# Hash attention with a squared-ReLU network on one core: the first pair of heads loads six tokens in a row per partition, transposes them by products, and the first weights' rounding moves to its usual place

## The chip, the cores and the metric

The kernel runs on one core of one Trainium2 chip. The metric is the device time of one execution in microseconds (us). Below, PE is TensorE, DVE is VectorE, ACT is ScalarE, POOL is GpSimd and SP is SyncE, as the profile names them; SPq and ACTq are transfers that SP and ACT issue. L396 is line 396 of the kernel.

## The reference

Attention for 4 batches of 8 heads, with 768 tokens of 64 features each. A token has six hash bits, the signs of its products with `proj`; a query attends only to keys with the same six bits.

```python
q_bits = (np.einsum('bhsd,dk->bhsk', q, proj) > 0)      # the same for k
mask = q_bucket[:, :, :, None] == k_bucket[:, :, None, :]
scores = np.where(mask, scale * np.matmul(q, k.T), -1e9)
attn = exp(scores - max) ; attn = attn / (sum(attn) + 1e-9)
x = (attn @ v), as 3072 tokens x 512 features
out = (maximum(x @ w_in, 0) ** 2) @ w_out                # 512 -> 2048 -> 512
```

`q`, `k`, `v` and `proj` are float32. `w_in` and `w_out` come as 64-bit floats and are rounded to float32 on the chip.

## The kernel before

The first part is the attention. It works through 16 pairs of heads; a pair fills 128 rows with its two heads' 64 features. The order of all instructions is written out by hand (`tc.manual_schedule()`), so each engine runs its instructions in the order of the text. The second part is the network. Its products run by a scheme with sums of blocks (L716, L888, L935), and it starts when the last pair is done. The first part holds about 317 us of the span.

One pair `pr` goes through these steps, and the names matter later:

- `load_pair` brings queries and keys of a pair (`q_nat`, `k_nat`) in 32-by-32 blocks. `features(pr, w)` transposes them on DVE (L333). `load_values` brings `v_nat`.
- `hash_bits` (L346) multiplies the features by the hash vectors on PE; `signs` (L356) makes the signs on ACT, 8 instructions a pair; `weigh` (L382) scales the key bits. `prepare` does hash and signs of the next pair. It is called inside `finish(pr - 1)`, after the second key tile of pair `pr`.
- `score(pr, kt)` computes the products of one key tile (128 keys) with all 768 queries: per column group, `bits` products and `feat` products accumulate in one tile of the pool `turn`, and one exponential on ACT (L413) takes them to `e`. A key tile has two column groups (512 and 256 queries, two heads each), thus two `turn` tiles and two exponentials. The pool has three buffers, shared by `score`, `hash_bits`, `sum_up` and the transposes of the first pair. A product that needs the fourth tile waits until the first has been read.
- `add_up` (L423, L428) sums the exponentials on DVE. `attend` (L438) multiplies them by the values. `sum_up`, `spread` and `normalize` end the pair; `finish(pr - 1)` runs the end of a pair inside the next one.

Between these steps the 64-bit network weights are rounded, two pieces per pair: `load_weight(i)` loads a piece (`raw`), `part_weight` splits its high word on DVE (L143, L147), `place_power` rebuilds the exponent on ACT (L160, L161), and `round_weight` puts it together on DVE (L171, L176, L179). In every pair but the first, `place_power(a)` and `round_weight(a)` of the even piece stand after the fourth key tile's exponentials. In pair 0 both stand behind the sixth key tile, after `weigh(1)`.

The first pair starts otherwise. `load_first` loads `q` and `k` in pieces of 128 tokens (token `t * 128 + p` on partition `p`), so a run in memory is one token, 256 bytes. `first_features(w, r)` transposes three pieces of both heads on PE, one 128 by 128 transpose each, and copies the result to `feat` (queries on ACT, L316; keys on DVE, L318). `keep_busy(n)` puts `n` unused products on PE (L326): eight before the first transposes and two between those of the queries and those of the keys. Then come the hash products, the signs of the queries on ACT, and `first_keys`, which makes the key bits on DVE (L370, L374).

Of the kernel before, what the change touches and what calls it, by code (L numbers as in the profile page):

```python
# [8 lines left out]
FP32 = mybir.dt.float32  # L9
# [25 lines left out]
def kernel(  # L35
# [10 lines left out]
    nc = tc.nc  # L46
    PSUM = bass.MemoryType.PSUM

    B, H, S, D = q.shape
# [3 lines left out]
    P = 128  # L53
    SB = S // P
    HS = S // 2
# [15 lines left out]
    ident = glob.tile([P, P], FP32, name="ident")  # L71
# [20 lines left out]
    p_qk = first.enter_context(tc.tile_pool(name="p_qk", bufs=2))  # L92
# [11 lines left out]
    def turn(name):  # L104

        return ps_s.tile([P, 2, 512], FP32, name=name, tag="turn")
# [11 lines left out]
    def goal(i):  # L118
        if i < 2 * NIN:
            return ins[i // NIN][:, i % NIN // 2, i % 2]  # L120
        return p_t.tile([P, DM], FP32, name="out_piece", bufs=3)
# [31 lines left out]
    def place_power(i):  # L153


        if i not in parts:
            return
        power = parts[i][0]
        small = p_w.tile([P, PIECE], U8, name="small")
        nc.scalar.activation(out=small, in_=power, func=ACTF.Relu, bias=excess)  # L160
        nc.scalar.activation(out=power, in_=small, func=ACTF.Copy, scale=2.0**23)  # L161

    def round_weight(i):

        raw = raws.pop(i, None)
        if raw is None:
            return keep_weight(i)
        goals[i] = goal(i)
        low, high = raw[:, :, 0], raw[:, :, 1]
        power, top = parts.pop(i)  # L170
        nc.vector.scalar_tensor_tensor(  # L171
            out=power, in0=high, scalar=0x80000000, in1=power,
            op0=ALU.bitwise_and, op1=ALU.bitwise_or,
        )
        one = top.bitcast(FP32)
        nc.vector.scalar_tensor_tensor(  # L176
            out=one, in0=low, scalar=2.0**-32, in1=top, op0=ALU.mult, op1=ALU.add,
        )
        nc.vector.scalar_tensor_tensor(  # L179
            out=goals[i], in0=one, scalar=2.0**-20, in1=power.bitcast(FP32),  # L180
            op0=ALU.mult, op1=ALU.mult,
        )
        keep_weight(i)

    def keep_weight(i):

        t = goals.pop(i)
        j, c = divmod(i, NIN)
        if j >= 2:
            nc.sync.dma_start(out=w_out_1[:, i - 2 * NIN], in_=t)  # L190
        elif c == NIN - 1:
            nf = NFT // 2
            for n, f, h in (0, 0, 0), (1, nf, 0), (2, nf, 1):
                put_factor(n, j * PIECE, ins[j][:, f:f + nf, h])
            nc.sync.dma_start(
                out=w_in_21[:, :, j * PIECE:(j + 1) * PIECE], in_=ins[j][:, 0:nf, 1]
            )
# [67 lines left out]
    nat, feat, bits = {}, {}, {}  # L265

    def load_first():

        for src, name in ((q, "q_nat"), (k, "k_nat")):
            t = p_qk.tile([P, SB, 2, D], FP32, name=name)  # L270
            for h, queue in enumerate((nc.sync, nc.scalar)):
                queue.dma_start(
                    out=t[:, :, h], in_=src[0, h].rearrange("(t p) d -> p t d", t=SB)
                )
            nat[0, name] = t
        for h, queue in enumerate((nc.sync, nc.scalar)):
            queue.dma_start(out=projs[h * D:(h + 1) * D, 0:NBITS], in_=proj)
# [15 lines left out]
    def load_values(pr):  # L293
        b, j = divmod(pr, PB)
        t = p_v.tile([P, 2, SB * D], FP32, name="v_nat")
        nc.sync.dma_start(
            out=t.rearrange("p h (t d) -> p (h t) d", d=D),
            in_=v[b, 2 * j:2 * j + 2].rearrange("h (t p) d -> p (h t) d", t=SB),
        )
        nat[pr, "v_nat"] = t  # L300

    def first_features(w, r):

        if r == 0:
            feat[0, w] = p_f.tile([P, S], FP32, name=f"feat{w}")
        tp = turn("tp")[:, 0]
        for i in range(SB // 2):
            t = r * (SB // 2) + i
            nc.tensor.transpose(  # L309
                out=tp[:, i * P:(i + 1) * P],  # L310
                in_=nat[0, ("q_nat", "k_nat")[w]][:, t].rearrange("p h d -> p (h d)"),
                identity=ident,
            )
        out = feat[0, w][:, r * HS:(r + 1) * HS]
        if w == 0:
            nc.scalar.copy(out=out, in_=tp[:, 0:HS])  # L316
        else:
            nc.vector.tensor_copy(out=out, in_=tp[:, 0:HS])  # L318

    busy = const.tile([P, 512], BF16, name="busy")  # L320
    void = ps_o.tile([P, 1024], FP32, name="xo")
# [1 line left out]
    def keep_busy(n, w=512):  # L323

        for _ in range(n):
            nc.tensor.matmul(  # L326
                out=void[:, 0:w], lhsT=busy[:, 0:P], rhs=busy[:, 0:w], start=True, stop=True
            )
# [8 lines left out]
    def hash_bits(pr, banks, ws=(0, 1), cs=(0, 1)):  # L337


        for w in ws:  # L340
            hashed[pr, w] = banks
            for c in cs:
                g = 2 * w + c
                for h in range(2):
                    rows = slice(h * D, (h + 1) * D)
                    nc.tensor.matmul(  # L346
                        out=banks[g * NR_B:(g + 1) * NR_B, h, 0:HS], lhsT=projs[rows],
                        rhs=feat[pr, w][rows, c * HS:(c + 1) * HS], start=True, stop=True,
                    )

    def signs(pr, w):
        bits[pr, w] = t = all_bits[pr % 2][w]
        for c in range(2):
            at = slice((2 * w + c) * NR_B, (2 * w + c + 1) * NR_B)
            for h in range(2):
                nc.scalar.activation(  # L356
                    out=t[h * D:h * D + NR_B, c * HS:(c + 1) * HS], in_=hashed[pr, w][at, h, 0:HS],
                    func=ACTF.Sign, scale=HUGE, bias=lifts[at],
                )
# [191 lines left out]
    def load_x(i):  # L551

        x = p_c.tile([P, NFT, NCH], FP32, name="x")
        nc.gpsimd.dma_start(out=x, in_=x_all[:, :, i * NCH:(i + 1) * NCH])
        xs[i] = x, [p_c.tile([P, 2, NCH // 2], FP32, name=f"t_x{n}") for n in range(3)]
# [36 lines left out]
    with tc.manual_schedule():  # L592
        nc.vector.memset(busy, 1.0)
        nc.vector.memset(projs, 0.0)
        load_first()
        keep_busy(8)
        make_identity(nc, ident)
        constants()
        load_pair(1)
# [2 lines left out]
            load_weight(i)  # L602
        first_features(0, 0)
        first_features(0, 1)
        keep_busy(2)
        first_features(1, 0)
        hash_bits(0, void.rearrange("p (h c) -> p h c", h=2), (0,))
        signs(0, 0)
# [5 lines left out]
        for pr in range(NP):  # L614
            a, b = 2 * pr, 2 * pr + 1
            more = pr + 1 < NP

            def prepare():

                hash_bits(pr + 1, turn("hash"))  # L620
                for w in (1, 0):
                    signs(pr + 1, w)


            if pr + 2 < NP:
                load_pair(pr + 2)
            if pr == X_0:
                load_x(0)
            if more and pr > 0:
                for w in range(2):  # L630
                    features(pr + 1, w)
            if pr > 0:
                round_weight(b - 2)
                load_weight(b)
                for m in sums.get(pr, ()):
                    sum_in(m)
            score(pr, 0)
            if pr == 0:
                first_keys(1, turn("hash"))
            score(pr, 1)  # L640
            if pr == 0:
                for w in range(2):
                    features(1, w)
            if pr > 0:
                finish(pr - 1, prepare if more else None)
            add_up(pr, 1)
            if pr > 0:
                normalize(pr - 1)


            if pr == X_0 + 1:
                for n in range(2):
                    load_unit(n)
            part_weight(a)
            score(pr, 2)
            if pr == 0:
                prepare()
            score(pr, 3)
            if more and pr > 0:
                weigh(pr + 1)  # L660
            if pr > 0:
                place_power(a)
            attend(pr, 0)
            attend(pr, 1)
            for kt in (2, 3):
                add_up(pr, kt)
            if more:
                load_values(pr + 1)


            if pr > 0:
                round_weight(a)
            part_weight(b)
            if more:
                load_weight(a + 2)
            score(pr, 4)
            score(pr, 5)
            if pr == 0:
                weigh(1)
                place_power(0)  # L680
                round_weight(0)
            place_power(b)
            attend(pr, 2)
            attend(pr, 3)
            add_up(pr, 4)
            add_up(pr, 5)
# [529 lines left out]
        for i in range(NCHUNK):  # L1216
            for s in range(NR):
                r = order(i * NR + s)
# [269 lines left out]
```

## Time and profile before

| | before |
|---|---|
| median of 3 runs | 884.32 us (882.99 to 885.01) |
| the profiled execution's own time | 884.32 us |
| its span | 882.6 us |
| mean granted TensorE clock | 0.993 |
| PE busy | 867.5 us (98% of the span) |
| DVE busy | 760.0 us (86%) |
| ACT busy | 391.5 us (44%) |

The span is the time from the first to the last instruction. It is 1.7 us shorter than the execution's own time; that remainder lies around the program. Busy shares are means over both parts of the kernel, so they don't say what bounds the short stretch in which the first pair runs. A row of a timeline gives the start, the length of a group of instructions, the engine, the line, the operation, the count, and in brackets how long the engine stood idle before it and what ended that.

### The profile page before, as it was taken

How to read it: one execution, taken by the hardware profiler on the slowest of the kernel's cores; microseconds unless marked ns; L12 is line 12 of the kernel's file. 1: busy time of each engine (PE TensorE's matmuls, PEld its weight loads, DVE VectorE, ACT ScalarE, POOL GpSimd, SP SyncE). 2: the span in 40 equal slices, each digit the busy share in tenths (PEclk: the TensorE clock that was granted, in tenths of full speed). 3: DMA queues.
4: the chain of work that ended last, by engine and by line, in shares of the span. 5: the costliest groups of instructions: out<-in, count | busy, mean ns of one | idle time of the engine just before them, and what ended most of it. 6: DMA issues, size and time to landing. Idle time of an engine off the chain costs nothing.

```text
span 882.6 us, 12133 instructions
## 1 busy us (share of the span) xinstructions
PE 867.5 (98%) x4340; PEld 520.6 (59%) x4340; DVE 760.0 (86%) x1099; ACT 391.5 (44%) x673; POOL 107.0 (12%) x172
## 2 busy tenths in 40 slices
PE   8899999999999999999999999999999999999996
PEld 4344444444444444444688875556888755568885
DVE  5799999999999998888779978888889788888875
ACT  6688888888888862222211123332111233321110
POOL 2000000000000000564222021111100211110002
PEclk9899999999999999999999999999999999999998
DMA  9567968899988634989897774436847744454565
GB/s 174 101 133 145 249 145 164 163 277 209 189 172 190 200 126 156 324 262 289 283 359 244 188 165 163 164 116 229 294 144 186 173 155 157 130 166 148 162 167 111
DMA packets 224131, 167.09 MB, mean 189 GB/s; under 512 B 164448, under 2 KB 181344, under 8 KB 224064
## 3 DMA queue, kind: packets, MB, share of 16 engines
q1 hardware_dynamic: 189152, 87.19, 41.1%
q0 software_dynamic: 12528, 41.30, 14.9%
q10 hardware_dynamic: 22384, 37.76, 14.2%
q8 instruction: 36, 0.59, 0.3%
q14 instruction: 31, 0.25, 0.1%
HBM read 124.52 MB, written 41.68 MB: 188 GB/s over the span
## 4 chain that ended last, share of the span: by engine, by line
PE 95%; DVE 2%; SPq 1%; DMA 1%; issue 0%; ACT 0%; DVEq 0%
PE acc L716 40%; PE st L396 16%; PE acc L935 16%; PE xo L438 13%; PE acc L888 5%; PE hash L346 2%; PE tot L455 1%; SPq L287 1%; DVE total L428 1%; DMA w_in<-s_in 1%; PE xo L326 0%; DMA raw<-in_moe_w_in_dram 0%; PE tp L309 0%; SPq L130 0%; PE xo L477 0%
## 5 line engine op out<-in xcount | busy, mean ns | idle before, releaser
L413 ACT ACTIVATE e<-st 128x1024 f32<-128x1024 f32 x192 | 145.0, 810 | 45.9 <-PE st L396 42.2
L396 PE MATMUL st<-feat,feat 64*128 64x512 f32 (+1 forms) x768 | 150.4, 484 | 0.0
L438 PE MATMUL xo<-e,v_nat 128*64 128x512 f32 (+1 forms) x768 | 136.0, 496 | 0.0
L716 PE MATMUL acc<-b,leaf 128*128 128x256 f32 x600 | 133.2, 379 | 0.5 <-issue 0.5
L716 PEld LDWEIGHTS acc<-b,leaf 128*128 128x128 f32 x600 | 113.9, 190 | 16.7 <-issue 1.5
L428 DVE TENSOR_TENSOR total<-total,e 128x1536 f32<-128x1536 f32 x64 | 112.4, 1756 | 8.4 <-ACT e L413 3.6
L438 PEld LDWEIGHTS xo<-e,v_nat 128*64 128x64 f32 x768 | 51.7, 137 | 83.5 <-issue 75.7
L935 PE MATMUL acc<-t_x,w_unit 128*128 128x512 f32 x192 | 90.2, 592 | 0.0
L396 PEld LDWEIGHTS st<-feat,feat 64*128 64x128 f32 x768 | 66.0, 188 | 32.9 <-issue 22.9
L716 PE MATMUL acc<-t,leaf 128*128 128x256 f32 x336 | 76.2, 380 | 0.0
L356 ACT ACTIVATE bits<-hash,lifts 32x384 bf16<-32x384 f32 x120 | 68.6, 572 | 6.7 <-PE hash L346 4.8
L716 PEld LDWEIGHTS acc<-t,leaf 128*128 128x128 f32 x336 | 63.7, 190 | 9.0 <-DVE t L516 0.5
L800 DVE SCALAR_TENSOR_TENSOR b<-h 128x512 f32<-128x512 f32 x96 | 65.7, 691 | 3.0
L396 PE MATMUL st<-bits,bits 64*128 64x256 bf16 (+1 forms) x384 | 63.1, 325 | 0.7 <-ACT bits L356 0.5
L935 PE MATMUL acc<-x,w_unit 128*128 128x512 f32 x128 | 60.1, 592 | 0.0
L716 PE MATMUL acc<-x,w_unit 128*128 128x512 f32 x128 | 56.5, 593 | 0.0
L716 PE MATMUL acc<-b_t,leaf 128*128 128x256 f32 x240 | 53.8, 379 | 0.0
L935 PEld LDWEIGHTS acc<-t_x,w_unit 128*128 128x128 f32 x192 | 36.5, 190 | 28.8 <-issue 26.8
L723 ACT COPY two<-acc 128x256 f32<-128x256 f32 (+1 forms) x29 | 12.5, 431 | 87.7 <-PE acc L716 78.4
L723 ACT COPY one<-acc 128x256 f32<-128x256 f32 (+1 forms) x29 | 12.5, 431 | 84.9 <-PE acc L716 41.9
L716 PEld LDWEIGHTS acc<-b_t,leaf 128*128 128x128 f32 x240 | 45.6, 190 | 6.1
L396 PEld LDWEIGHTS <-bits 64*128 64x128 bf16 x384 | 23.5, 93 | 41.5 <-issue 37.4
(159 smaller groups left out, 1168.6 us busy)
## 6 DMA issues: line engine op xcount, KB each, us to landing
leaf<-w_out ACTq DMA_DIRECT2D x142, 256.0 KB, 3.1
w_unit<-w_in SPq DMA_DIRECT2D x16, 640.0 KB, 4.0
raw<-in_moe_w_in_dram SPq DMA_DIRECT2D x16, 512.0 KB, 5.6
raw<-in_moe_w_out_dram SPq DMA_DIRECT2D x16, 512.0 KB, 4.4
w_unit<-w_in SPq DMA_DIRECT2D x8, 896.0 KB, 8.3
w_out<-sums POOLq DMA_DIRECT2D x16, 448.0 KB, 6.8
sum<-w_in SPq DMA_DIRECT2D x16, 448.0 KB, 4.8
v_nat<-in_v_dram SPq DMA_DIRECT2D x16, 384.0 KB, 4.5
```

The source lines that it names most:

```text
L287: nc.sync.dma_start(out=t[g * 32:(g + 1) * 32].rearrange("i (c d) -> i c d", d=32), in_=src[b, 2 * j + h].rearrange("(c i) (e d) -> e i c ...
L346: nc.tensor.matmul(out=banks[g * NR_B:(g + 1) * NR_B, h, 0:HS], lhsT=projs[rows], rhs=feat[pr, w][rows, c * HS:(c + 1) * HS], start=True, ...
L356: nc.scalar.activation(out=t[h * D:h * D + NR_B, c * HS:(c + 1) * HS], in_=hashed[pr, w][at, h, 0:HS], func=ACTF.Sign, scale=HUGE, bias=li ...
L396: nc.tensor.matmul(out=st[:, h, 0:hi - lo], lhsT=src[pr, 1][rows, key], rhs=src[pr, 0][rows, lo:hi], start=first, stop=not first,)
L413: nc.scalar.activation(out=e[:, :, lo:hi], in_=sts[i][:, :, 0:hi - lo], func=ACTF.Exp, scale=scale)
L428: nc.vector.tensor_tensor(out=totals[pr], in0=totals[pr], in1=weights[pr, kt][:, :, 0:S], op=ALU.add)
L438: nc.tensor.matmul(out=xo[h * D:(h + 1) * D, lo:hi], lhsT=nat[pr, "v_nat"][:, h, kt * D:(kt + 1) * D], rhs=weights[pr, kt][:, h, lo:hi], s ...
L716: nc.tensor.matmul(out=acc[to], lhsT=a(i), rhs=b(i), start=first and i == 0, stop=last and i == n - 1, skip_group_check=True,)
L723: nc.scalar.copy(out=t, in_=acc[of])
L800: nc.vector.scalar_tensor_tensor(out=out, in0=h, scalar=0.0, in1=h, op0=ALU.max, op1=ALU.mult)
L888: nc.tensor.matmul(out=out, lhsT=w[:, a], rhs=b, start=start, stop=stop, skip_group_check=True)
L935: nc.tensor.matmul(out=acc[to], lhsT=w[:, PLACE[a], f], rhs=bt[b](f), start=first and f == 0, stop=last and f == NFT // 2 - 1, skip_group_ ...
```

## The change

Four things change, all in the first pair.

1. `load_first` and, for pair 0, `load_values` put tokens `6 p` to `6 p + 5` on partition `p`. A run in memory is then six tokens, 1536 bytes. Keys and values have the same new order, so the sums over keys are the same. The queries are put back in order by the copy after the transposes, which writes every sixth element.
2. `first_features` makes, for each piece, two products with the identity (one per head, 64 output rows each) in place of one transpose. The second half of the queries is copied by DVE and not by ACT.
3. Six unused products stand ahead of the transposes (eight before), and none between queries and keys (two before).
4. In pair 0, `place_power(0)` and `round_weight(0)` stand where the other pairs have them: `place_power(0)` after the exponentials of the fourth key tile, and `round_weight(0)` ahead of `part_weight(1)`.

```diff
     def load_first():
         for src, name in ((q, "q_nat"), (k, "k_nat")):
-            t = p_qk.tile([P, SB, 2, D], FP32, name=name)
+            t = p_qk.tile([P, 2, SB, D], FP32, name=name)
             for h, queue in enumerate((nc.sync, nc.scalar)):
                 queue.dma_start(
-                    out=t[:, :, h], in_=src[0, h].rearrange("(t p) d -> p t d", t=SB)
+                    out=t[:, h], in_=src[0, h].rearrange("(p t) d -> p t d", t=SB)
                 )
...
     def load_values(pr):
+        if pr == 0:
+            nc.sync.dma_start(out=t, in_=v[0, 0:2].rearrange("h (p t) d -> p h (t d)", t=SB))
+        else:
...
     def first_features(w, r):
...
-            nc.tensor.transpose(
-                out=tp[:, i * P:(i + 1) * P],
-                in_=nat[0, ("q_nat", "k_nat")[w]][:, t].rearrange("p h d -> p (h d)"),
-                identity=ident,
-            )
-        out = feat[0, w][:, r * HS:(r + 1) * HS]
+            for h in range(2):
+                nc.tensor.matmul(
+                    out=tp[h * D:(h + 1) * D, i * P:(i + 1) * P],
+                    lhsT=nat[0, ("q_nat", "k_nat")[w]][:, h, t], rhs=ident, start=True, stop=True,
+                )
         if w == 0:
-            nc.scalar.copy(out=out, in_=tp[:, 0:HS])
+            (nc.vector.tensor_copy if r else nc.scalar.copy)(
+                out=feat[0, w].rearrange("f (p t) -> f t p", t=SB)[:, r * (SB // 2):(r + 1) * (SB // 2)],
+                in_=tp[:, 0:HS].rearrange("f (t p) -> f t p", p=P),
+            )
         else:
-            nc.vector.tensor_copy(out=out, in_=tp[:, 0:HS])
+            nc.vector.tensor_copy(out=feat[0, w][:, r * HS:(r + 1) * HS], in_=tp[:, 0:HS])
...
-        keep_busy(8)
+        keep_busy(6)
...
         first_features(0, 1)
-        keep_busy(2)
         first_features(1, 0)
...
-            if pr > 0:
-                place_power(a)
+            place_power(a)
             attend(pr, 0)
...
-            if pr > 0:
-                round_weight(a)
+            round_weight(a)
             part_weight(b)
...
             if pr == 0:
                 weigh(1)
-                place_power(0)
-                round_weight(0)
             place_power(b)
```

More of the change, by code (lines that the diff above doesn't have):

```diff
@@ L295, in load_values @@
         t = p_v.tile([P, 2, SB * D], FP32, name="v_nat")
-        nc.sync.dma_start(
-            out=t.rearrange("p h (t d) -> p (h t) d", d=D),
-            in_=v[b, 2 * j:2 * j + 2].rearrange("h (t p) d -> p (h t) d", t=SB),
-        )
+        if pr == 0:
+            nc.sync.dma_start(out=t, in_=v[0, 0:2].rearrange("h (p t) d -> p h (t d)", t=SB))
+        else:
+            nc.sync.dma_start(
+                out=t.rearrange("p h (t d) -> p (h t) d", d=D),
+                in_=v[b, 2 * j:2 * j + 2].rearrange("h (t p) d -> p (h t) d", t=SB),
+            )
         nat[pr, "v_nat"] = t
@@ L308, in first_features @@
             t = r * (SB // 2) + i
-            nc.tensor.transpose(
-                out=tp[:, i * P:(i + 1) * P],
-                in_=nat[0, ("q_nat", "k_nat")[w]][:, t].rearrange("p h d -> p (h d)"),
-                identity=ident,
-            )
-        out = feat[0, w][:, r * HS:(r + 1) * HS]
-        if w == 0:
-            nc.scalar.copy(out=out, in_=tp[:, 0:HS])
+            for h in range(2):
[3 more added lines that the diff above has]
+                )
+        if w == 0:
+            (nc.vector.tensor_copy if r else nc.scalar.copy)(
+                out=feat[0, w].rearrange("f (p t) -> f t p", t=SB)[:, r * (SB // 2):(r + 1) * (SB // 2)],
+                in_=tp[:, 0:HS].rearrange("f (t p) -> f t p", p=P),
+            )
         else:
-            nc.vector.tensor_copy(out=out, in_=tp[:, 0:HS])
+            nc.vector.tensor_copy(out=feat[0, w][:, r * HS:(r + 1) * HS], in_=tp[:, 0:HS])
     busy = const.tile([P, 512], BF16, name="busy")
```

## The prediction

> **What bounds the kernel now.** I read the page first, then PE's timeline around the first pair, the clock by windows there, and the timelines of DVE and ACT in the same stretch. The page says that PE is the bound:
>
> ```profile
> PE 867.5 (98%) x4340; PEld 520.6 (59%) x4340; DVE 760.0 (86%) x1099; ACT 391.5 (44%) x673; POOL 107.0 (12%) x172
> ```
>
> So a gain must come from the 15 us in which PE is idle, or from stretches in which it is slow. PE's timeline has one large hole, where pair 1 waits for the features of pair 2:
>
> ```profile
> 30.62 0.39 PE L396 MATMUL st<-feat,feat 64*128 64x256 f32 x2
> 34.60 2.27 PE L346 MATMUL hash<-feat,projs 64*32 64x384 f32 x16 [3.58 <-DVE feat L333]
> 36.81 1.51 PE L455 MATMUL tot<-total,ones 128*32 128x384 f32 x8
> 38.24 3.97 PE L438 MATMUL xo<-e,v_nat 128*64 128x512 f32 x16
> ...
> 42.23 0.39 PE L396 MATMUL st<-bits,bits 64*128 64x512 bf16 x2
> ```
>
> The same sequence one pair later has no hole, and its rows are shorter:
>
> ```profile
> 57.73 0.88 PE L346 MATMUL hash<-feat,projs 64*32 64x384 f32 x16
> 58.53 0.85 PE L455 MATMUL tot<-total,ones 128*32 128x384 f32 x8
> 59.31 2.81 PE L438 MATMUL xo<-e,v_nat 128*64 128x512 f32 x16
> ...
> 62.13 0.39 PE L396 MATMUL st<-bits,bits 64*128 64x512 bf16 x2
> ```
>
> The table by windows tells why they are longer in pair 1 (the columns after the window: its length, busy time of PE, PEld, DVE, ACT, POOL, then the granted clock). After the hole the clock is at half speed for 6.8 us:
>
> ```profile
> 31.00:33.80 2.80, 0.02 (x2) 0.00 (x0) 2.77 (x3) 1.13 (x2) 0.00 (x0) 1.00 0.81 206
> 33.80:40.60 6.80, 6.00 (x32) 1.56 (x34) 5.46 (x9) 3.57 (x7) 0.00 (x0) 0.50 0.01 2
> ```
>
> From the end of pair 1's second key tile (31.0) to the third's start (42.23) pass 11.2 us; from 57.73 to 62.13 pass 4.4. The hole and its cold clock cost 6.8 us. Nothing gives them back: the third key tile comes 19.90 us later in the next pair (42.23 to 62.13), and pairs 2 to 3 have the same distance in the chain (62.20 to 82.11).
>
> Who is late? DVE's rows:
>
> ```profile
> 28.09 0.69 DVE L171 SCALAR_TENSOR_TENSOR power<-raw,power 128x512 uint32<-128x512 uint32 x1 [2.77 <-ACT power L161]
> ...
> 30.03 3.54 DVE L428 TENSOR_TENSOR total<-total,e 128x1536 f32<-128x1536 f32 x2
> 33.49 0.97 DVE L333 STREAM_TRANSPOSE feat<-q_nat 128x768 f32<-128x768 f32 x1
> 34.38 0.94 DVE L333 STREAM_TRANSPOSE feat<-k_nat 128x768 f32<-128x768 f32 x1
> ```
>
> DVE is idle 2.77 us until ACT has done `place_power(0)`; then `round_weight(0)`, two sums and the two transposes follow without a pause. ACT does it late, behind the last six exponentials and `weigh(1)`:
>
> ```profile
> 21.32 4.51 ACT L413 ACTIVATE e<-st 128x1024 f32<-128x1024 f32 x6
> 25.85 0.94 ACT L382 ACTIVATE bits<-bits,gains 128x768 bf16<-128x768 bf16 x1
> 26.69 0.71 ACT L160 ACTIVATE small<-power,excess 128x512 uint8<-128x512 uint32 x1
> ```
>
> The chain of waits puts the stretch before the transposes on a transfer of `raw` that lands at 33.45. I don't believe it: the transpose doesn't read `raw`, and DVE is busy with the sums until 30.03 + 3.54 = 33.57. Neighbours on DVE overlap by 0.08 (33.49 + 0.97 against 34.38), so 33.49 is just the end of the sums.
>
> **Part 4, the moved weight steps.** On ACT, `place_power(0)` goes in after the fourth tile's two exponentials, which end at about 22.8. Its two instructions take 1.27 us (26.69 to 27.96, where the next pair of them starts). It is done at 24.1, and the next exponential starts there in place of 22.75. ACT's total is the same, so pair 1's first exponential keeps its place at 29.24. Queued behind the moved step are the exponentials of tiles five and six. PE waits for them through the three `turn` buffers: the last column group of tile six starts at 24.03 now, and needs the buffer that tile five's first exponential reads. That one takes 1.01 (the 1024-element form at 29.24) and ends at 25.05, so PE goes on at 25.15: +1.1 us. Some 0.15 of it is won back at 30.30, where PE waits a little for ACT today (1.03 after the row before it, against 0.86 for the same step at 28.51). PE thus ends the second key tile at 31.95. Term: +0.95.
>
> On DVE, the sum of the fourth tile still runs from 22.86 to 24.6. `round_weight(0)` is ready at 24.1, so it starts at 24.55 and takes 1.94 (28.09 to 30.03): 26.5. `part_weight(1)` takes 0.7: 27.2. The two sums take 3.46 (30.03 to 33.49) and their exponentials have ended by 27.1: 30.6. The transposes then end at 31.6 (queries) and 32.4 (keys), 2.9 us earlier than now. PE arrives at 31.95 and needs the keys' features 0.45 us into the hash products: it waits about 0.1 to 0.4. The hole is gone, and what is left is too short for the clock to fall, which today falls 2.8 us into the hole. Terms: -6.8 and +0.3. No transfer moves with these steps: `round_weight(0)` issues none, and it frees a `raw` buffer 3 us earlier for a load that SP reaches only at 29.8.
>
> Sum of part 4: -6.8 + 0.95 + 0.3 = **-5.55 us**.
>
> **Parts 1 to 3, the start.** PE's rows now:
>
> ```profile
> 1.48 3.60 PE L326 MATMUL xo<-busy 128*128 128x512 bf16 x8 [1.48 <-DVE excess L235]
> 4.87 1.49 PE L309 MATMUL tp<-ident,q_nat 128*128 128x128 f32 x6
> 6.15 0.77 PE L326 MATMUL xo<-busy 128*128 128x512 bf16 x2
> 6.76 0.51 PE L309 MATMUL tp<-ident,k_nat 128*128 128x128 f32 x3
> 7.22 0.95 PE L346 MATMUL xo<-feat,projs 64*32 64x384 f32 x8
> ```
>
> The unused products are 0.427 us apart at 1.48 and 0.22 at 6.54, so PE runs at half speed until about 6.4, though this column of the profile shows a full clock there. Two of them fewer ahead save 0.85 us if the queries have landed by 4.06. They land 3.3 (SP) and 3.9 us (ACT) after issues at 0.77, at 4.66. With a sixth of the runs they should be earlier, by anything between 0 and 1 us; the nearest row is a 256 KB load of 2 KB rows, `leaf`, with 3.1 us, thus 3.9, and I take 4.06: the unused products set the start. The two between save 0.6 more if the keys, which hold PE today (landed at 6.7), come by then; I take that, since all of their traffic has a sixth of the runs.
>
> **Their products** stand against this. Six transposes leave six records, but four hash products leave eight: a float32 product is two passes. So 24 passes with 24 weight loads of 64 columns replace 6 transposes for the queries, and 12 replace 3 in each half of the keys. A pass of 128 columns lasts 0.213 at half clock (transposes at 4.87) and 0.107 to 0.12 at full. The two heads write different rows and overlap, as `attend`'s do: 16 records, 8 of 512 and 8 of 257 columns, in 2.7 us. That makes 0.107 and 0.055 per pass if the moving side sets the pace; the weight loads follow each other by 0.075 at full clock (four in 0.36 for L477) and maybe 0.15 at half. Queries: 24 x 0.107 to 0.15 = 2.6 to 3.6 against 1.28, ending at 6.6 to 7.1 with the clock rising at 6.4. First keys: 12 x 0.055 to 0.075 = 0.7 to 0.9 against 0.46. Hash products then start at 7.3 to 8.0, against 7.22. The second half of the keys adds 0.2 to 0.45. The start costs +0.3 to +1.3, and I take **+0.8**, nearer to the load-bound end, since `attend` with its longer passes doesn't show short ones overlapping.
>
> The copies lie beside this. ACT's first copy (0.48) runs under the second half of the query products. DVE's new copy (0.56 for 384 elements in a row, L318) ends before the keys' products do; at twice that it costs nothing to 0.5. No row shows a copy that writes every sixth element, so I take the plain one's time and keep the double as the other end. [...] DVE has nothing else queued behind it until the keys' copy.
>
> The unused products also warm the clock. The granted clock falls at 33.8 and returns at 40.6, and the start warms near 6.45: all three are multiples of 3.4 us apart. [...]
>
> The values' load is needed at 18.05 and lands near 14: nothing.
>
> **The sum.** -5.55 + 0.8 = -4.75. The profiled execution's own time is 884.32 us (span 882.6 and 1.7 around it), which is also the median of the runs: **879.6 us**. What a measurement can tell from no change is about 0.2%, 1.77 us: faster means under 882.55.
>
> **The rivals.** *Dear products (slower).* The 48 passes at the start stand in line, each behind its own weight load: 24 x (0.231 + 0.213) and 24 x (0.141 + 0.107) = 16.6 us, against 2.2 for the transposes and 1.4 saved. Start +13, total +7.4: 891.8. It turns the sign beyond no change from 0.23 us per pass on. For it: no short float32 pass onto 64 rows, one after another, is in the trace but for L477. Against it: `attend` and L477 overlap their passes. Chance 0.04.
>
> *The hole stays.* The chain is right, and the features of pair 2 wait for a transfer at about 33.45. Then hash starts at 34.6 as now, and the start's cost is swallowed: 884.3, or 881.3 if the clock survives the shorter hole (2.65 us). Chance 0.06.
>
> *A cold start.* [...] Chance 0.12.
>
> **How the numbers follow.** The forecast has 0.78. Its own range goes from 877.4 (start -0.4, if loads land early and the clock rises with them; part 4 at -6.5, if the 0.95 or most of it is hidden) to 881.1 (start +1.8, the 1.3 and a doubled copy; part 4 at -5.0, if 0.5 more of the hole is left). The three runs lie 2 us apart, so I put 0.2 more below: 877.2. Upwards the range reaches to 882.5 to take in most of the cold start; outside are the other two rivals and the rest of it. Faster: 0.78 + 0.08 + 0.02 = 0.88; within 0.2%: 0.08; slower: 0.04.
>
> **What would show it.** Right: DVE's L171 of piece 0 starts near 24.5 to 25.5, no wait of 2.77 there; the hash products of pair 2 follow the second key tile with under 0.5 us idle; the clock stays full from 30 to 45; third key tile of pair 1 near 37.3. The last products of tile six come 1 us later after tile five. At the start, hash products near 8.0. Wrong: idle over 2 us before L346's second group, query products over 4 us, or a pair distance other than 19.9.

## The result, and the profile after

The changed kernel takes 880.16 us (median of 6 runs, 878.87 to 881.27); the kernel before, beside it, 884.64 us (6 runs). The ratio is 0.9953 with a 95% interval of 0.9939 to 0.9967, so it is 0.3% to 0.6% faster. The forecast was 879.6 us, in a range of 877.2 to 882.5.

The page's first line hardly differs. PE has 1.9 us less busy time in a span that is 4.1 us shorter:

```profile
span 878.5 us, 12193 instructions
PE 865.6 (99%) x4372; PEld 521.1 (59%) x4372; DVE 760.8 (87%) x1100; ACT 391.7 (45%) x672; POOL 106.9 (12%) x172
```

PE's timeline of the changed kernel, from the end of pair 1's second key tile (its last row first) to the third tile's first products. Line numbers are 6 higher than before:

```profile
32.14 0.60 PE L402 MATMUL st<-feat,feat 64*128 64x256 f32 x4
32.66 1.47 PE L352 MATMUL hash<-feat,projs 64*32 64x384 f32 x16
34.06 0.85 PE L461 MATMUL tot<-total,ones 128*32 128x384 f32 x8
34.84 2.81 PE L444 MATMUL xo<-e,v_nat 128*64 128x512 f32 x16
...
37.66 0.39 PE L402 MATMUL st<-bits,bits 64*128 64x512 bf16 x2
```

The hole of 3.58 us is gone; no bracket stands behind the hash products. They take 1.47 in place of 0.88, since the products of the keys have to wait for their features. The rows for the sums and the values are as short as a pair later. In the same window in which the clock was at half speed, it is now full (length, busy time of PE, PEld, DVE, ACT, POOL, clock):

```profile
33.80:40.60 6.80, 6.80 (x56) 3.21 (x52) 6.56 (x12) 6.12 (x11) 0.00 (x0) 1.00 0.00 0
```

DVE's rows show why. The rounding of the first weights follows a sum without the 2.77 us wait, and the queries' features are made at 31.40, not at 33.49:

```profile
25.27 0.68 DVE L171 SCALAR_TENSOR_TENSOR power<-raw,power 128x512 uint32<-128x512 uint32 x1
...
27.87 3.61 DVE L434 TENSOR_TENSOR total<-total,e 128x1536 f32<-128x1536 f32 x2
31.40 0.97 DVE L339 STREAM_TRANSPOSE feat<-q_nat 128x768 f32<-128x768 f32 x1
32.29 0.94 DVE L339 STREAM_TRANSPOSE feat<-k_nat 128x768 f32<-128x768 f32 x1
```

ACT's rows show the moved step in its new place, and PE's row of the sixth key tile what it costs there. The exponentials that were to follow at 23.6 start at 24.87, and PE waits 0.99 us for them:

```profile
22.05 1.51 ACT L419 ACTIVATE e<-st 128x1024 f32<-128x1024 f32 x2
23.58 0.72 ACT L160 ACTIVATE small<-power,excess 128x512 uint8<-128x512 uint32 x1
24.34 0.63 ACT L161 ACTIVATE power<-small 128x512 uint32<-128x512 uint8 x1
24.87 2.90 ACT L419 ACTIVATE e<-st 128x1024 f32<-128x1024 f32 x4
```

```profile
25.93 0.29 PE L402 MATMUL st<-bits,bits 64*128 64x256 bf16 x2 [0.99 <-ACT e L419]
```

At the start, PE's rows are:

```profile
1.48 2.74 PE L332 MATMUL xo<-busy 128*128 128x512 bf16 x6 [1.48 <-DVE excess L235]
4.15 2.83 PE L314 MATMUL tp<-ident,q_nat 128*64 128x128 f32 x24
6.77 0.98 PE L314 MATMUL tp<-ident,k_nat 128*64 128x128 f32 x12
7.98 0.85 PE L352 MATMUL xo<-feat,projs 64*32 64x384 f32 x8 [0.23 <-issue]
```

The queries land 2.8 to 3.0 us after their issue, and the keys 3.5 to 3.9 us (before: 3.3 to 3.9, and 4.4 to 5.4). So neither holds PE up. The hash products start at 7.98 (7.22 before), and the second key tile at 12.90 (12.17).

### The profile page after: what moved, and what is told of

It reads as the page before. It is cut to its first block, busy times and chain, and to the rows that moved or that the text cites. A ratio compares the mean times of both kernels' runs of the same rounds, so it can differ in the third digit from the quotient of the medians.

```text
span 878.5 us, 12193 instructions
## 1 busy us (share of the span) xinstructions
PE 865.6 (99%) x4372; PEld 521.1 (59%) x4372; DVE 760.8 (87%) x1100; ACT 391.7 (45%) x672; POOL 106.9 (12%) x172
## 4 chain that ended last, share of the span: by engine, by line
PE 96%; DVE 2%; ACT 1%; issue 0%; DVEq 0%; ACTq 0%
PE acc L717 40%; PE st L402 17%; PE acc L936 16%; PE xo L444 14%; PE acc L889 6%; PE hash L352 2%; PE tot L461 1%; DVE total L434 1%; ACT bits L362 1%; PE tp L314 0%; ACT e L419 0%; PE xo L332 0%; PE xo L483 0%; DVE x_t L499 0%; DVE recs L493 0%
## 5 line engine op out<-in xcount | busy, mean ns | idle before, releaser
L402 PEld LDWEIGHTS <-bits 64*128 64x128 bf16 x384 | 23.6, 93 | 42.5 <-issue 38.3
```

Of the source, the lines that this page charges most:

```text
L402: nc.tensor.matmul(out=st[:, h, 0:hi - lo], lhsT=src[pr, 1][rows, key], rhs=src[pr, 0][rows, lo:hi], start=first, stop=not first,)
```

## The experiments

My theory: all of the gain is part 4, and its two halves are the hole and the half clock after it; the start costs somewhat. The rivals: the gain comes from the start; the long rows after the hole are only waits; the start's loads or its unused products matter by themselves.

One number serves for all runs: the distance from the first product of pair 0's second key tile to that of pair 1's third, in the one profile of each run. Being a difference, it leaves out the start. It doesn't leave out how long the clock stays low behind the hole, which differs from run to run: 6.8 us in the profile before, 3.4 in e2_start_only. The time's ratio is against runs of the kernel before that were measured beside it.

| run | second key tile | third, pair 1 | distance | median us | ratio (95%) |
|---|---|---|---|---|---|
| before | 12.17 | 42.23 | 30.06 | 884.64 | |
| changed | 12.90 | 37.66 | 24.76 | 880.16 | 0.9953 (0.9939 to 0.9967) |
| e1_move_only | 12.51 | 37.28 | 24.77 | 879.58 | 0.9949 (0.9933 to 0.9966) |
| e2_start_only | 11.98 | 41.16 | 29.18 | 884.66 | 1.0008 (0.9998 to 1.0017) |
| e3_fill_hole | 12.17 | 39.76 | 27.59 | 882.78 | 0.9983 (0.9973 to 0.9992) |
| e5_late_round | 12.35 | 36.06 | 23.71 | 878.61 | 0.9934 (0.9918 to 0.9951) |
| e4_plain_copy | 12.12 | 36.87 | 24.75 | 879.27 (one run) | |
| e6_short_runs | 14.89 | 39.67 | 24.78 | 881.43 | 0.9972 (0.9962 to 0.9981) |
| e7_old_busy | 13.23 | 37.99 | 24.76 | 881.60 | 0.9968 (0.9958 to 0.9979) |
| e8_both | 12.96 | 36.66 | 23.70 | 878.42 | 0.9936 (0.9919 to 0.9952) |
| e9_split_rounds | 12.03 | 35.22 | 23.19 | 878.85 | 0.9942 (0.9926 to 0.9959) |
| e10_after_again | 11.96 | 36.71 | 24.75 | 879.89 | 0.9953 (0.9936 to 0.9969) |

**Part 4 alone (e1_move_only).** The kernel before, with these lines as the changed kernel has them:

```diff
-            if pr > 0:
-                place_power(a)
+            place_power(a)
...
-            if pr > 0:
-                round_weight(a)
+            round_weight(a)
...
                 weigh(1)
-                place_power(0)
-                round_weight(0)
```

> The kernel before with part 4 alone (the first weights' exponent and rounding in their usual place); its start is as before. If the hole and its half clock are what the change removes: the hash products of pair 2 follow pair 1's second key tile with under 0.5 us idle, the clock stays full, and the third key tile of pair 1 starts near 36.9 us (42.23 before), so 5.3 us faster, near 879.3 us. If the gain of the change comes from its start (parts 1 to 3): the third key tile stays near 42 and the time near 884.

Measured: distance 24.77, 5.29 less than in the profile before and the same as in the changed kernel; 879.58 us, by the ratio 4.5 us faster (3.0 to 5.9). The whole gain is here, and the rival that puts it in the start falls.

**Parts 1 to 3 alone (e2_start_only).** The changed kernel with those lines put back.

> Parts 1 to 3 alone (loads, products, copies, fewer unused products); the weights' steps stay late, as before. If the start costs what the two traces show: the second key tile starts 0.73 us later (12.90 against 12.17), the hole and the half clock are there as before, third key tile of pair 1 near 43.0, time near 885.4. If the start is what gains: under 883.

Measured: 884.66 us, and an interval that holds no change. The hole is there as before. But the second key tile came earlier than before (11.98), not 0.73 later, and the half clock after the hole was shorter. The windows of this run (columns as above):

```profile
33.80:35.80 2.00, 1.38 (x16) 0.34 (x16) 2.00 (x4) 0.00 (x0) 0.00 (x0) 1.00 0.00 0
35.80:39.30 3.50, 3.50 (x18) 0.81 (x16) 2.77 (x6) 3.09 (x6) 0.00 (x0) 0.51 0.02 5
39.30:41.00 1.70, 1.70 (x16) 0.82 (x14) 1.10 (x1) 1.49 (x3) 0.00 (x0) 1.00 0.00 0
```

Here the clock is low for 3.4 us, and not for 6.8 as in the profile before, and it falls when PE has already worked again for 1.4 us (since 34.42). So the same hole has two prices: the distance is 29.18 here and 30.06 in the profile before. The mean granted clock is 0.996 in this profile and 0.993 in that one; of the 43 runs of the kernel before that were measured beside the experiments, 29 have 0.995 or more and 14 have 0.994 or less. If these are the same two cases, the kernel before mostly pays the lower price, and the profile before shows the rarer, dearer one. The expected figure for the start, too, was one draw of the time at which PE comes to full speed. Two runs of one and the same kernel make this plain below (e10_after_again).

**The hole filled (e3_fill_hole).** The kernel before, with unused products in the hole:

```diff
         tot = turn("tot")
+        if pr == 0:
+            for _ in range(12):
+                nc.tensor.matmul(
+                    out=tot[:, 0], lhsT=busy[:, 0:P], rhs=busy, start=True, stop=True
+                )
```

> The kernel before with twelve unused products (2.6 us at full clock) in the hole ahead of the hash products of pair 2. DVE still ends the features at 34.4. If the half clock after the hole is a cost of its own: the granted clock stays full from 31 to 41, the rows of hash, tot and xo are as short as one pair later, third key tile near 39.5, 2.7 us faster than before. If the long rows after the hole are waits on other engines: third key tile near 42.2, no gain.

PE's rows of this run:

```profile
34.61 1.62 PE L346 MATMUL hash<-feat,projs 64*32 64x384 f32 x16 [0.89 <-DVE feat L333]
36.15 0.85 PE L455 MATMUL tot<-total,ones 128*32 128x384 f32 x8
36.94 2.81 PE L438 MATMUL xo<-e,v_nat 128*64 128x512 f32 x16
```

The features came no earlier, and the hash products start at 34.61 as before. Yet the rows behind them are short, the clock stays full (1.00 from 31.0 to 40.6), and the third key tile comes at 39.76: 2.47 us won by work that nobody uses. So of the 5.29 between the profiles about half is the half clock, and the rest the hole itself. The time fell by 1.5 us (0.7 to 2.4). This is nearer to the price of a low stretch of 3.4 us: from the first hash product to the third key tile it is 5.15 us here, 6.74 in e2_start_only and 7.63 in the profile before, so the half clock costs 1.6 or 2.5.

**Another way to end the hole (e5_late_round).** Only DVE's order changes; ACT's steps stay late:

```diff
+            if pr == 1:
+                round_weight(0)
             if pr > 0:
                 round_weight(b - 2)
...
                 place_power(0)
-                round_weight(0)
```

> The kernel before; only round_weight(0) moves, from ahead of the last two sums of pair 0 to behind the features of pair 2 on DVE; place_power(0) stays late on ACT, so the fifth and sixth key tiles' exponentials aren't held up. If the cause of the hole is DVE's order alone: the sums run from 25.2, the features end by 30.5, PE has no wait at the hash products nor at the sixth key tile, and the third key tile of pair 1 starts near 35.7, 6.6 us before that of the kernel before and 1.2 ahead of part 4 alone, near 878.0 us. If the two roundings in a row behind the features hold up the row sums' transpose instead: a wait at the products with picks, third key tile at 36.5 or later.

Measured: distance 23.71, 1.06 less than with part 4; 878.61 us. PE waits neither at the sixth key tile nor at the hash products. The rival is there in small: with two roundings in a row ahead of the row sums' transpose, PE waits for `both`:

```profile
35.82 0.30 PE L477 MATMUL xo<-both,picks 128*64 128x24 f32 x4 [0.30 <-DVE both L466]
```

**The strided copies (e4_plain_copy).** The changed kernel with the queries' copies in a row:

```diff
-                out=feat[0, w].rearrange("f (p t) -> f t p", t=SB)[:, r * (SB // 2):(r + 1) * (SB // 2)],
-                in_=tp[:, 0:HS].rearrange("f (t p) -> f t p", p=P),
+                out=feat[0, w][:, r * HS:(r + 1) * HS], in_=tp[:, 0:HS],
```

> The changed kernel with the two copies of the queries written in a row and not to every sixth element; it thereby leaves out putting the first pair's queries back in order. If the step of six elements is what makes the two copies 0.85 us long: they take 0.48 on ACT and 0.56 on DVE, as the copies in a row do, the hash products follow the keys' products with no wait (0.23 now), and the time falls by about 0.25, which one run can't show. If reading two products' halves or the partition order is what makes them long: still 0.85.

First the two copies of the changed kernel (ACT, then DVE), then those of this run:

```profile
5.75 0.85 ACT L319 COPY feat<-tp 128x384 f32<-128x384 f32 x1 [2.18 <-PE tp L314]
7.03 0.85 DVE L319 COPY feat<-tp 128x384 f32<-128x384 f32 x1 [3.75 <-PE tp L314]
```

```profile
5.70 0.48 ACT L319 COPY feat<-tp 128x384 f32<-128x384 f32 x1 [2.13 <-PE tp L314]
6.36 0.56 DVE L319 COPY feat<-tp 128x384 f32<-128x384 f32 x1 [3.09 <-PE tp L314]
```

Writing every sixth element makes a copy of 384 elements 0.85 us on either engine, against 0.48 and 0.56. The wait of 0.23 ahead of the hash products is gone with it.

**Short runs on the tile's side (e6_short_runs).** The tile of before, one transpose per piece, tokens still six in a row in memory:

```diff
-            t = p_qk.tile([P, 2, SB, D], FP32, name=name)
+            t = p_qk.tile([P, SB, 2, D], FP32, name=name)
...
-                    out=t[:, h], in_=src[0, h].rearrange("(p t) d -> p t d", t=SB)
+                    out=t[:, :, h], in_=src[0, h].rearrange("(p t) d -> p t d", t=SB)
...
-            for h in range(2):
-                nc.tensor.matmul(
-                    out=tp[h * D:(h + 1) * D, i * P:(i + 1) * P],
-                    lhsT=nat[0, ("q_nat", "k_nat")[w]][:, h, t], rhs=ident, start=True, stop=True,
-                )
+            nc.tensor.transpose(
+                out=tp[:, i * P:(i + 1) * P],
+                in_=nat[0, ("q_nat", "k_nat")[w]][:, t].rearrange("p h d -> p (h d)"),
+                identity=ident,
+            )
```

> The changed kernel with the tile of queries and keys as before (both heads of a token side by side) and one transpose per piece in place of two products; tokens stay six in a row in memory, but in the tile a run is one token, 256 bytes. If the products are what the start pays for, and the loads come as early as with the long runs: six transposes take 1.3 us from 4.15, the hash products start near 6.5, 1.5 us before those of the changed kernel, time near 878.8. If short runs on the tile's side make the loads as slow as before: queries land near 4.7, keys near 6.7, the hash products start near 7.4 to 8.0, time within 0.5 us of the changed kernel's 880.2.

The loads are as slow as before (keys 4.7 and 5.5 us to landing, against 3.5 to 3.9): only the runs that are long on both sides came early. And the start is much worse than either theory had it:

```profile
5.09 1.51 PE L313 MATMUL tp<-ident,q_nat 128*128 128x128 f32 x6 [0.88 <-POOL which L260]
7.14 0.87 PE L313 MATMUL tp<-ident,k_nat 128*128 128x128 f32 x3 [0.53 <-DMA k_nat<-in_k_dram]
...
10.92 2.61 PE L402 MATMUL st<-feat,feat 64*128 64x512 f32 x8
```

The last row takes 1.56 in the changed kernel. PE paused twice, for 0.88 and 0.53 us, and its products stayed at half speed until about 13. In the two profiles of the changed kernel, where PE has no pause ahead of these products, they come to full speed at about 7.1 and 5.1. This is the cold start that the prediction names among its rivals. The second key tile is 2.0 us later than in the changed kernel's slower profile, and the median time is 1.3 us higher. The run doesn't price the cold start alone, since it also has transposes in place of the products. (The first bracket names POOL, which had long been done; by the landing times it is the queries, issued at 0.8 and 4.2 us under way.)

**The unused products (e7_old_busy).** The changed kernel with `keep_busy(8)` and, between queries and keys, `keep_busy(2)`.

> The changed kernel with eight and two unused products, as before. If the unused products only stand in the way: the queries' products start at 4.9 in place of 4.15 and the keys' wait for two more, so the first key tile starts 1.0 to 1.4 later, time near 881.3. [...]

881.60 us, 1.4 above the changed kernel (ratio 0.9968 against 0.9953, with overlapping intervals, so the times alone don't decide it). The second key tile starts at 13.23, later than in either profile of the changed kernel (12.90 and 11.96). So here, where the queries land 3.0 to 3.2 us and the keys 3.5 to 4.0 us after their issue, the products that stand in for the loads only cost.

**Both (e8_both), the roundings apart (e9_split_rounds), the changed kernel again (e10_after_again).** The first is the changed kernel with the weights' steps of e5_late_round. The second is e5_late_round with one step moved:

```diff
             if pr == 1:
                 round_weight(0)
-            if pr > 0:
+            if pr > 1:
                 round_weight(b - 2)
...
                 normalize(pr - 1)
+            if pr == 1:
+                round_weight(1)
```

> The changed kernel with the weights' steps as in the run with the late rounding (place_power(0) behind the last exponentials, round_weight(0) behind the features of pair 2). If part 4's 0.95 us (the sixth key tile's wait for ACT) and its rest of the hole can be had without touching the start: no wait at the sixth key tile, no wait at the hash products, third key tile of pair 1 some 1.1 us earlier than in the changed kernel, time 1.1 below that of the changed kernel in this call, and 0.6 above the late rounding with the old start. If the new start has used up the slack of DVE: same time as the changed kernel.

> The kernel before with round_weight(0) behind the features of pair 2 and round_weight(1) behind the normalizing of pair 0, so that the two don't stand in a row ahead of the row sums' transpose. If that row was what PE waited 0.30 us for at the products with picks: the wait is gone, third key tile of pair 1 near 35.8, time near 878.3. If DVE is full through pair 1: the 0.3 comes back as a later hash of pair 3, time 878.6 as with the late rounding.

> The changed kernel once more, beside the two above on the same chip: 880.2, third key tile of pair 1 at 37.7, give or take half a microsecond by where the clock's window falls at the start.

The first gives 878.42 us against 879.89 for the changed kernel measured beside it, with a distance of 23.70: the late rounding is worth the same on either start. It lies 0.2 below the old start's 878.61, not 0.6 above; a difference of this size is within the spread of the runs. The second wins the 0.30 and more (distance 23.19), but loses it in the next pair, where the features of pair 3 come later and the hash products wait for them (0.88 elsewhere):

```profile
50.72 1.60 PE L346 MATMUL hash<-feat,projs 64*32 64x384 f32 x16
```

DVE makes these features at 49.58 and 50.48, with no wait in its rows since 36: it is full, as the rival said. The time is 878.85.

The third shows how much of the start is chance. PE's rows of this run, to be held against 2.83 and 0.98 of the first profile:

```profile
4.15 1.96 PE L314 MATMUL tp<-ident,q_nat 128*64 128x128 f32 x24
5.95 0.82 PE L314 MATMUL tp<-ident,k_nat 128*64 128x128 f32 x12
```

The same 24 passes from the same start take 0.8 us less, since PE comes to full speed two microseconds earlier: the time for two passes falls from 0.213 to 0.109 us at about 5.1 here, and at about 7.1 in the first profile. (This is what the expectation speaks of as the clock's window.) The second key tile comes at 11.96 and not at 12.90.

The versions e5_late_round and e8_both beat the kernel before clearly. Against the versions with part 4 their distance is 1.1 us shorter, and their medians are 1.0 us (e5_late_round against e1_move_only) and 1.5 us lower (e8_both against e10_after_again), though the intervals of their ratios overlap. With 4 runs each the two can't be told apart.

## Why the prediction was right

**Part 4: forecast -5.55, measured -5.29 between the profiles and -4.5 by the times.** The mechanism is the one that was forecast. Nothing later takes the gain back: the network's first product, too, lies 5.3 us nearer to the second key tile than in the profile before. Term by term:

- The hole and its clock, -6.8. The hole is gone and the clock full. e3_fill_hole shows that the clock was a cost of its own, 2.47 of it. But -6.8 is the price with a clock that stays low for 6.8 us. With the 3.4 us of e2_start_only the distance falls by 4.4 only, which is close to the 4.5 of the times (3.0 to 5.9). I took one profile's draw of the clock for the cost of every run; for a run in which it stays low for 3.4 us the term is some 0.9 too large.
- PE's wait for ACT at the sixth key tile, +0.95 net of what pair 1 wins back. The wait is 0.99; the last column group of tile six comes 1.17 later after the one before it, and pair 1 wins back 0.17, which leaves +1.00. (Pair 1's first exponential doesn't keep its place at 29.24, as I had it: with the shift of the start taken off it begins at 29.89 and waits for PE. No term hung on it.) e5_late_round, which lacks it and the wait for the keys' features, is 1.06 better, although it adds 0.30 elsewhere.
- The rest of the hole, +0.3. The hash products take 1.47 in place of 0.88: +0.59. Both ends came as worked out: with the start's shift of 0.73 taken off, PE arrives at 31.93 (forecast 31.95) and the keys' features end at 32.5 (32.4). What I had wrong is when PE needs them. I had it use the queries' features alone for 0.45 us. The records of the single products show that one pair later the first eight of the sixteen start within 0.05 us, those of the queries and of the keys side by side. In the changed kernel four start at 32.66 and four at 33.01, all on the queries, and the eight on the keys only from 33.28. So what is lost is the running side by side, 0.6 us.

That the total of 879.6 came within 0.6 us of the measured 880.16 is partly luck: by the times part 4 gained about 1.0 less than I said, and the start, by the figures below, cost less than 0.8.

**The reading of the chain.** The transposes of pair 2 waited for DVE's order and not for the load that the chain named: in e1_move_only they start at 31.02 with that load issued as late as ever (29.83) and landing 4.8 us after it. The rival of the hole that stays had no other support.

**The start: forecast +0.8, measured -0.2 to +0.7.** The profile shows +0.73, but the right size can't be read from one profile. The second key tile starts at 12.03 to 12.51 in the five runs with the old start and at 11.96 to 12.96 in the four with the new one (before and e1, e3, e5, e9; changed and e2, e8, e10): 12.25 and 12.45 on average. Runs in which the clock rises, by the spacing of the products, at about the same time compare better. Where it rises before 5.5, the tile starts at 12.03 with the old start (e9) and at 11.96 and 11.98 with the new (e10, e2); where it rises after 7.0, at 12.51 (e1) and at 12.90 and 12.96 (changed, e8). So the new start costs nothing or some 0.4 us, depending on when the clock rises; that rests on these six profiles. The times say +0.55 (e2_start_only, -0.2 to +1.5), +0.6 and +0.3 (the changed kernel's two medians against e1_move_only), and -0.2 (e8_both against e5_late_round); none of these is clear of the noise. Inside the start, two terms were off in opposite ways. The product passes are cheaper than I took them: 24 in 2.62 us is 0.109 at half clock. At full, 12 up to the start of the next group take 0.8, which is 0.067, and while they follow each other two take 0.109. So passes that follow each other have the pace that the prediction worked out from `attend`'s (0.107 and 0.055), not its slower one by the weight loads (0.15 and 0.075). And the copies cost 0.85, near the other end of what I had bounded, so that the hash products wait 0.23 for DVE.

For the copies I had taken the plain one's time and kept the double as the other end. Steps of six took 0.85 in place of 0.48 (ACT) and 0.56 (DVE), nearer to the double; what that cost on the path is 0.23 (0.34 in e10_after_again).

**The clock.** I took 6.4 from the profile before as the time at which PE comes to full speed. That was one draw: the changed kernel has it at about 7.1 and at about 5.1 in two profiles, though in both the queries' products start at 4.15. The fall isn't tied to the length of the idleness alone either. In the profile before it came 2.8 us after the last product, with PE still idle, and in e2_start_only after 3.59 us of idleness and 1.4 us of new work. The clock stayed low for 6.8 us (33.8 to 40.6) in the first and for 3.4 (35.9 to 39.3) in the second. No run shows what sets these times.

**The rivals.** Dear products: 0.067 to 0.109 per pass, far from 0.23. The hole stays: no. A cold start: not in the changed kernel, whose queries landed in time (2.8 to 3.0 us after their issue), but in e6_short_runs, where they didn't (3.3 and 4.2). The upper end of the range counts on a cold start with a price of +2.5. That was my estimate and no run shows it; e6_short_runs has 2.0 at the second key tile and 1.3 in the median time, both against the changed kernel and with the transposes in them. Nor does a run show that the clock rises with early loads, on which the -0.4 of the lower end rests.

**What stays open.** The network part doesn't take the same time in every run: from its first product to the end of the span it was 546.2 us in the profile before (336.37 to 882.6), 546.7 in the changed kernel's (331.81 to 878.5) and 547.9 in its second (330.85 to 878.7); over all twelve profiles it lies between 546.2 and 548.1. The change doesn't touch it. This is why the spans differ by 4.1 us where the third key tiles are 4.57 apart, and why differences of a microsecond between medians of few runs decide little here. The cause is open. (The first of these products also shows that the first part holds 336 us in the profile before, and not the 317 given at the beginning.)

## What to carry to other kernels

When PE waits for a few microseconds, look at the granted clock behind the wait as well: here a hole of 3.6 us cost another 1.6 or 2.5 in half-speed products. Follow the waiting engine back through its own order to the first idle time, which may lie on a third engine, here ACT doing a step of no urgency before one that DVE stood waiting for; reordering DVE alone was better still than doing the step early. And measure a change of a microsecond at the start over many runs, or between profiles in which PE comes to full speed at the same time, because that time isn't the same in each run (about 7.1 and 5.1 us in two profiles of one kernel here). The same goes for the price of a hole behind which the clock is low: one profile is one draw of it (here 3.4 or 6.8 us at half clock).

## What the runs showed of the hardware that was not expected

- The clock can fall when PE is already at work again: in e2_start_only at about 35.9, with products since 34.42. It then stays low for 3.4 us there, and for 6.8 in the profile before, which costs 1.6 and 2.5 us.
- The profile's clock column shows 1.00 from the start in the profiles of the kernel before and the changed one, while the unused products are 0.427 us apart, and 0.22 later in the profile before. In e6_short_runs it shows 1.00 from 9 to 13 us, where the score products take 2.61 us in place of 1.56. At the start, the spacing of the products is the better measure.
- A load whose runs are six tokens long in memory but one token long in the tile is as slow as one with short runs on both sides: the keys land 5.5 us (SP's queue) and 4.7 us (ACT's) after their issue in e6_short_runs, 4.4 and 5.4 in the kernel before, and 3.5 and 3.9 with long runs on both sides.
